# A fused attention-and-feed-forward kernel on one core: lower-triangle score pieces, the first tile's h units moved, and the last two output tiles from seven block products

## The chip, the cores and the metric

The kernel runs on one core of a Trainium2 chip. The metric is the device time of one execution in microseconds; the time before is 1198.16 us, the median of 8 runs (1196.76 to 1198.74). One further execution was taken with the hardware profiler on; its trace is what is read here.

## The reference, cut to what matters

```python
# u, v: (8, 3008, 256); z: (8, 3008, 64); w_in: (256, 2048); w_out: (2048, 256); all float32
scores = (1 / S) * matmul(z, z.T)              # per batch, S = 3008; symmetric
attn   = maximum(scores, 0) ** 2               # symmetric too
x      = u * matmul(attn, v)                   # (8 * 3008, 256)
h      = x @ w_in                              # (24064, 2048)
out    = (h * cos(h)) @ w_out                  # (24064, 256)
```

## The kernel before, in words

**Slots and tiles.** Each of the 8 batches has 3008 rows, cut into 6 column blocks J of 512 (the last has 448). A slot s is one (batch, J), 48 in all. The feed-forward part works on tiles m of 512 rows of x, 48 as well (of every two batches, the first one's last block keeps 384 rows as its tile and hands 64 to the second one's, which makes 512, in the buffer `xodd`). The order of the instructions on each engine is written out by hand (`manual_schedule`); the engines run their queues in that order, and waits follow from the data and from the buffers.

**Phase a of slot s** (`phase_a`, L305; `phase_a_first`, L347, for the first three) computes the attention output of the slot: 47 pairs of matmuls for each of the two halves `dh` of the 256 columns (`emit_value`, L257). A pair's two matmuls contract 64 rows each: t = 0 uses rows 0 to 63 of the PE array (half 0), t = 1 rows 64 to 127 (half 1), into different PSUM banks. Between the value pairs lie the score groups of later slots.

**A score group** (`emit_score`, L182) is again a pair of 64-row matmuls, with z transposed as both operands: t = 0 on half 0, t = 1 on half 1, each W columns wide, into the two banks of a PSUM pair E (three such pairs in turn, `take_e`). ACT then takes max(., 0) of both (L204), DVE squares it into a piece A (L209, L212). A piece is a 512 by 512 block (J, I) of attn; two groups, h = 0 and h = 1, make one. Since attn is symmetric, only pieces with I >= J are computed (apart from the first three slots of batch 0) and the others are turned by DMA transposes (`emit_turns`, L226, on SP's queue, L244). Of a diagonal piece (I = J, `cut` at L185) the group h = 0 is computed 256 columns wide, h = 1 at full width; the two missing 128-row blocks are turned from the piece itself by two transposes (L238).

**Phase b of slot s** (`phase_b`, L565) is the feed-forward part: eight h units of tile s - 1 (`emit_h`, L396: four 128-row matmuls, then a Sin on ACT, L411, then h times cos(h) into g on DVE, L414), and between them the output y of tile s - 2. There are two buffers of g, so that g of tile m takes the place of g of tile m - 2. For most tiles (`mixed`, L418: 1 <= m < 46 and 512 rows) y is made from seven products of half-size blocks instead of eight (a Strassen-like scheme): the sums and differences s1 and g are made on POOL (`mix_early`, L424, two instructions for each of four j), s2 and s4 on DVE (`mix_late`, L431) in the next phase a, and each product (`product`, L450) is 16 matmuls 128 columns wide into one of the two banks M0 and M1, which ACT (products 1 and 5) or DVE (the others) empties. The other tiles use 64 matmuls of 256 columns (`emit_y`, L515, `store_y`, L533). The last tile's y stands after everything (`last_y`, L544): its four 128-row blocks one after the other, each copied by ACT (L554) into an output buffer o (two in turn) and stored by SP (L560, L562; the last 64 rows by ACT's queue, L563).

**The beginning** (L597 to L685): batch 0's z is turned on PE (`turn_on_pe`, L618) in six groups, and copied out of PSUM by ACT or DVE (`copy_turned`, L625). The last two groups are turned within phase a of slot 0, at its steps 4 and 8 (`turn_late`, L669, L681). After the sixth, its PSUM space becomes the third pair E. The first two h units of tile 0 stand between phases a of slots 1 and 2 (L684, L685), the other six in phase b of slot 2. w_out is loaded after slot 1 (L683), on POOL's queue behind a small instruction (`hold`, L344) that waits for that slot's sums.

Of the kernel before, what the change touches and what calls it, by code (L numbers as in the profile page):

```python
# [14 lines left out]
def kernel(  # L15
# [9 lines left out]
    nc = tc.nc  # L25
# [155 lines left out]

    def emit_score(on_dve=False, later=None):  # L182
        b, J, I, h = groups[done_groups[0]]
        done_groups[0] += 1
        cut = I == J and not (b == 0 and J < 3)  # L185
        W = 2 * P if cut and h == 0 else width(J)
        zT = zTs[b]
        e = E[take_e()]
        for t in range(2):
            k = 4 * I + 2 * h + t  # L190
            nc.tensor.matmul(  # L191
                e[:, t, 0:W],
                zT[t * H:(t + 1) * H, k * P:(k + 1) * P],
                zT[t * H:(t + 1) * H, J * CW:J * CW + W],
                start=True,
                stop=True,
            )
        key = (b, J, I)
        a = new_piece(key) if h == 0 else piece(key)
        r = rpool.tile([P, 2, CW], FP16, name="r")  # L200
        if on_dve:
            nc.vector.tensor_scalar(r[:, :, 0:W], e[:, :, 0:W], 0.0, None, ALU.max)
        else:
            nc.scalar.activation(r[:, :, 0:W], e[:, :, 0:W], AF.Relu)  # L204
        def square():
            if I > J:
                a4 = a.rearrange("p (k t j) -> p t k j", k=4, j=P)[:, 2 * h:2 * h + 2, :, :]
                r4 = r.rearrange("p t (k j) -> p t k j", j=P)
                nc.vector.tensor_tensor(a4, r4, r4, ALU.mult)  # L209
            else:  # L210
                a4 = a.rearrange("p (k w) -> p k w", w=CW)[:, 2 * h:2 * h + 2, 0:W]
                nc.vector.tensor_tensor(a4, r[:, :, 0:W], r[:, :, 0:W], ALU.mult)  # L212

        if later is None:
            square()
        else:
            later.append(square)
        if h == 0:
            return
        if cut or (I > J and (b, J, I) not in direct):  # L220
            turns.append(((b, I), key))
            turns.sort(key=lambda t: t[0])
            turn_slots[key] = pieces[key]
            pending[pieces[key]] = "held"

    def emit_turns(due, more=0):  # L226
        while turns and (turns[0][0] <= due or more > 0):
# [6 lines left out]
            if I == J:  # L234
                a4 = a.rearrange("p (k w) -> p k w", w=CW)
                for rr in range(2, 4):
                    rows = P if J * 4 + rr < NB - 1 else H
                    nc.sync.dma_start_transpose(  # L238
                        a4[:, 0:2, rr * P:rr * P + rows],
                        a[0:rows, rr * CW:rr * CW + 2 * P],  # L240
                    )
            else:
                d = new_piece((b, I, J))
                nc.sync.dma_start_transpose(d.rearrange("p (n j) -> p n j", j=P), a)  # L244
# [102 lines left out]
    def phase_a_first(s, n, extra={}):  # L347
# [16 lines left out]
        for i, (dh, k) in enumerate(steps):  # L364
# [19 lines left out]
            for _ in range(at.get(i, 0)):  # L384
                emit_score(on_dve=done_groups[0] in on_dve)
        if s == 0:
# [31 lines left out]
    def mixed(m):  # L418
        return 1 <= m < NSLOT - 2 and mwidth(m) == CW

    F = NFT // 2
    T = 2 * P

    def mix_early(m, j):  # L424
        g, f = gs[m], slice(2 * j, 2 * j + 2)
        lower = slice(F + 2 * j, F + 2 * j + 2)
        nc.gpsimd.tensor_tensor(s1[:, f, :], g[:, f, T:], g[:, lower, T:], ALU.add)  # L427
        nc.gpsimd.tensor_tensor(g[:, f, T:], g[:, f, 0:T], g[:, f, T:], ALU.subtract)  # L428

# [19 lines left out]

    def product(m, n):  # L450
        g = gs[m]
# [9 lines left out]
        }[n]  # L461
        acc = M[order_y.index(n) % 2][:, 0:T]
        for ft in range(F):
            for k in range(2):
# [5 lines left out]
                    stop=(ft == F - 1 and k == 1),  # L470
                )
        acc = acc.rearrange("p (k d) -> p k d", d=P)
        if n == 5:
            y_outs[m] = [opool.tile([P, 2, D], FP32, name="o") for i in range(2)]
            y_parts[m] = {}
        c11, c12, c21, c22 = (y_outs[m][i][:, :, d * P:(d + 1) * P] for i in range(2) for d in range(2))
        parts = y_parts[m]
        add = lambda dst, other: nc.vector.scalar_tensor_tensor(
            dst, acc, inv_s2, other, ALU.mult, ALU.add
        )  # L480
        if n in (1, 5, 6):
            parts[n] = ypool.tile([P, 2, P], FP32, name=f"p{n}")
        if n in (1, 5):
            nc.scalar.activation(parts[n], acc, AF.Copy, bias=0.0, scale=inv_s2)
        elif n == 6:
# [14 lines left out]
    def y_bank(m, k):  # L500
        if m == NSLOT - 1 and k == 3:
            return E[0][:, 0, 0:D]
        return M[k // 2][:, (k % 2) * D:(k % 2 + 1) * D]

    def y_block(m, ft, k):
        final = m == NSLOT - 1
        nc.tensor.matmul(  # L507
            y_bank(m, k),
            gs[m][:, ft, k * P:(k + 1) * P],
            w_out16[:, ft, :],  # L510
            start=(ft == 0 and (k % 2 == 0 or (final and k == 3))),
            stop=(ft == NFT - 1 and (k % 2 == 1 or k == mwidth(m) // P - 1 or (final and k == 2))),
        )
# [30 lines left out]
    def last_y(m):  # L544
        b, J = m // NC, m % NC
        for ft in range(NFT):
            y_block(m, ft, 0)
            y_block(m, ft, 1)
        for k in range(4):
            if k >= 2:  # L550
                for ft in range(NFT):
                    y_block(m, ft, k)
            o = opool.tile([P, 2, D], FP32, name="o")
            nc.scalar.activation(  # L554
                o[:, 0, :], y_bank(m, k),
                AF.Copy, bias=0.0, scale=inv_s2,
            )
            t0 = b * S + J * CW + k * P
            if k < 3:
                nc.sync.dma_start(out[t0:t0 + P, :], o[:, 0, :])  # L560
            else:
                nc.sync.dma_start(out[t0:t0 + H, :], o[0:H, 0, :])  # L562
                nc.scalar.dma_start(out[b * S - H:b * S, :], o[H:P, 0, :])  # L563

    def phase_b(s):  # L565
        y, hs = s - 2, [(s - 1, i) for i in (0, 4, 1, 5, 2, 6, 3, 7)]
        if s == 2:
            hs = [(0, i) for i in range(2, 8)] + hs
        for dh in range(len(late_sums)):
            gate_mul(s, 2 - len(late_sums), late_sums.pop(0), nc.gpsimd)  # L570
        if mixed(y):
            ys = [lambda n=n: product(y, n) for n in order_y]
        else:
            ys = [lambda i=i: emit_y(y, i) for i in range(8)]
            ys[7] = lambda f=ys[7]: (f(), store_y(y))
        n = len(hs)
        if n > 8:
            after = (1, 2, 4, 5, 7, 8, 10, 11)
        elif mixed(y):
            after = range(7)  # L580
        else:
            after = (0, 1, 2, 3, 4, 5, 6, 6)
        for i, (m, unit) in enumerate(hs):
            times_c = emit_h(m, unit)
            if not mixed(y):
# [4 lines left out]
            if mixed(y):  # L590
                times_c()
            if mixed(m) and unit >= 4:
                mix_early(m, unit - 4)
            if i in (1, 3, 5):
# [44 lines left out]
    for g in range(3, NC):  # L639
        cast_z(nc.gpsimd, g)  # L640
        if g == 3:
            load_v(0, 1)
    on_dve = ()
    squares = []
# [24 lines left out]
    def turn_late(g):  # L669
        turn_on_pe(g)  # L670
        copy_turned(g)
        if g == NC - 1:
            E.append(ppool.tile([P, 2, CW], FP32, name="E2", tag="E2"))
            e_order.insert(0, 2)
# [8 lines left out]
    nc.gpsimd.dma_start(w_out16, moe_w_out.rearrange("(k p) f -> p k f", p=P))  # L683
    for i in range(2):  # L684
        emit_h(0, i)()  # L685
    phase_a_first(2, 14)
# [65 lines left out]
```

## Time and profile before

| | |
|---|---|
| median of 8 runs | 1198.16 us (1196.76 to 1198.74) |
| the profiled execution's own time | 1199.09 us |
| its span in the trace | 1197.3 us |
| granted PE clock | 1.0 throughout |
| phase a / phase b of a full slot, late in the run | 10 to 12 us / 13 us |
| last h unit of tile 47, first of its four matmuls | 1184.30 us |
| last store issued (L562) | 1194.08 us |

The span counts from the first to the last instruction of the program; the 1.8 us between it and the execution's own time lie outside the program. PE, DVE, ACT, POOL and SP are the engines (TensorE, VectorE, ScalarE, GpSimd, SyncE); PEld is PE's weight loads, SPq and ACTq the instructions by which an engine starts DMAs. In the timeline a line has the start in us from the span's start, the length in us, engine, line of the kernel, operation, output and inputs, shape, count, and in brackets the idle time before it and what ended that.

### The profile page before, as it was taken

Reading aid. Unit: us, or ns where it says so; the run is one execution under the profiler, and the core shown is the slowest. Engines: PE = TensorE matmul, PEld = TensorE weight load, DVE = VectorE, ACT = ScalarE, POOL = GpSimd, SP = SyncE. Lnnn points to the kernel's source line nnn. Section 1 sums busy time; section 2 is a strip of 40 time slices with the busy share of each in tenths; the row PEclk is TensorE's granted clock in tenths of the full one; section 3 lists DMA queues with packets and bytes.
Section 4 is the critical chain, followed back from the end, with each engine's and each line's share of the span. In section 5 each row is a group of like instructions: output and inputs, shape, how many; then the busy total and the mean of one; then the engine's idle time right before and its main releaser. Section 6 shows DMA issues by size and latency. Waiting matters only on the chain.

```text
span 1197.3 us, 28444 instructions
## 1 busy us (share of the span) xinstructions
PE 1187.7 (99%) x11743; PEld 703.3 (59%) x11743; DVE 996.9 (83%) x1257; ACT 795.1 (66%) x923; POOL 654.0 (55%) x667
## 2 busy tenths in 40 slices
PE   8999999999999999999999999999999999999998
PEld 4456656655556556655566555665566555656566
DVE  6888887889988897888988889788888888878775
ACT  7866676667766676666676676666766666676454
POOL 3196725557466571655647556276565665535450
PEclk9999999999999999999999999999999999999999
DMA  9999999568995699946999369973798838954301
GB/s 158 170 175 149 127 145 131 101 111 135 133 144 88 120 137 152 125 82 111 151 151 128 79 104 158 168 111 69 118 164 146 120 67 119 177 109 81 62 19 54
DMA packets 467411, 145.14 MB, mean 121 GB/s; under 512 B 391760, under 2 KB 467024, under 8 KB 467280
## 3 DMA queue, kind: packets, MB, share of 16 engines
q1 hardware_dynamic: 368304, 110.11, 51.7%
q0 software_dynamic: 97440, 32.78, 27.2%
q8 instruction: 92, 1.51, 0.5%
q10 hardware_dynamic: 1536, 0.43, 0.2%
q14 instruction: 39, 0.32, 0.1%
HBM read 66.32 MB, written 24.64 MB: 76 GB/s over the span
## 4 chain that ended last, share of the span: by engine, by line
PE 95%; DMA 2%; issue 1%; ACT 1%; DVE 0%; POOL 0%; ACTq 0%; SPq 0%; POOLq 0%
PE E L403 27%; PE M L465 21%; PE M L258 20%; PE E L258 18%; PE E L191 5%; PE M L507 3%; DMA w_out<-in_moe_w_out_dram 1%; ACT r L204 1%; DMA out_dram<-o 0%; PE E L635 0%; POOL u L140 0%; ACT o L554 0%; DVE A L209 0%; DVE A L212 0%; DVE sm L270 0%
## 5 line engine op out<-in xcount | busy, mean ns | idle before, releaser
L411 ACT ACTIVATE c<-E 128x1024 f16<-128x1024 f32 (+1 forms) x384 | 385.4, 1006 | 221.4 <-PE E L403 218.9
L414 DVE SCALAR_TENSOR_TENSOR g<-E,c 128x1024 f16<-128x1024 f32 (+1 forms) x384 | 458.7, 1196 | 74.7 <-ACT c L411 74.1
L204 ACT ACTIVATE r<-E 128x512 f16<-128x512 f32 (+1 forms) x342 | 327.7, 966 | 115.2 <-PE E L191 110.2
L258 PEld LDWEIGHTS <-v 64*128 64x128 f16 x4512 | 225.4, 94 | 252.5 <-issue 19.3
L403 PE MATMUL E<-x,w_in 128*128 128x512 f16 (+1 forms) x1408 | 354.0, 375 | 0.0
L427 POOL TENSOR_TENSOR s<-g 128x512 f16<-128x512 f16 x164 | 192.3, 1172 | 172.1 <-DVE g L414 132.6
L258 PE MATMUL M<-A,v 64*128 64x512 f16 (+1 forms) x2256 | 283.3, 372 | 0.3 <-DVE sm L270 0.3
L258 PE MATMUL E<-A,v 64*128 64x512 f16 (+1 forms) x2256 | 278.0, 372 | 0.0
L428 POOL TENSOR_TENSOR g<-g 128x512 f16<-128x512 f16 x164 | 203.2, 1239 | 12.9
L403 PEld LDWEIGHTS <-w_in 128*128 128x128 f16 x1536 | 134.4, 98 | 109.3 <-issue 19.5
L209 DVE TENSOR_TENSOR A<-r 128x1024 f16<-128x1024 f16 x240 | 173.4, 734 | 20.6 <-ACT r L204 19.8
L286 POOL TENSOR_TENSOR x<-sm,uT 128x512 f16<-128x512 f32 (+1 forms) x43 | 48.6, 1130 | 244.7 <-DVE sm L270 244.5
L465 PEld LDWEIGHTS <-g 128*128 128x128 f16 x2624 | 160.3, 98 | 37.0
L465 PEld LDWEIGHTS <-s 128*128 128x128 f16 x1968 | 120.2, 98 | 27.7
L191 PE MATMUL E<-zT 64*128 64x512 f16 (+2 forms) x684 | 126.2, 362 | 2.1 <-DVE zT L630 1.1
L433 DVE TENSOR_TENSOR s<-s,g 128x1024 f16<-128x1024 f16 x82 | 93.2, 1136 | 2.1 <-POOL s L427 2.1
L212 DVE TENSOR_TENSOR A<-r 128x512 f16<-128x512 f16 (+1 forms) x102 | 79.0, 774 | 13.9 <-ACT r L204 13.3
L465 PE MATMUL M<-w_mix,s 128*128 128x128 f16 x1312 | 86.6, 219 | 0.0
L465 PE MATMUL M<-w_out,g 128*128 128x128 f16 x1312 | 86.6, 219 | 0.0
L465 PE MATMUL M<-w_mix,g 128*128 128x128 f16 x1312 | 86.6, 219 | 0.0
L191 PEld LDWEIGHTS <-zT 64*128 64x128 f16 x684 | 35.6, 94 | 42.0 <-issue 4.4
L435 DVE TENSOR_TENSOR s<-g,s 128x1024 f16<-128x1024 f16 x82 | 55.9, 684 | 0.0
(55 smaller groups left out, 676.1 us busy)
## 6 DMA issues: line engine op xcount, KB each, us to landing
out_dram<-o SPq DMA_DIRECT2D x87, 256.0 KB, 2.2
v<-in_v_dram POOLq DMA_DIRECT2D x40, 256.0 KB, 7.7
u<-in_u_dram POOLq DMA_DIRECT2D x40, 256.0 KB, 4.9
A<-A SPq DMA_TRANSPOSE x207, 5.7
z<-in_z_dram POOLq DMA_DIRECT2D x14, 192.0 KB, 10.0
z<-in_z_dram POOLq DMA_DIRECT2D x14, 176.0 KB, 5.9
v<-in_v_dram POOLq DMA_DIRECT2D x8, 192.0 KB, 11.0
u<-in_u_dram POOLq DMA_DIRECT2D x8, 192.0 KB, 4.0
```

The lines of the kernel that those rows point to most:

```text
L191: nc.tensor.matmul(e[:, t, 0:W], zT[t * H:(t + 1) * H, k * P:(k + 1) * P], zT[t * H:(t + 1) * H, J * CW:J * CW + W], start=True, stop=True,)
L204: nc.scalar.activation(r[:, :, 0:W], e[:, :, 0:W], AF.Relu)
L209: nc.vector.tensor_tensor(a4, r4, r4, ALU.mult)
L212: nc.vector.tensor_tensor(a4, r[:, :, 0:W], r[:, :, 0:W], ALU.mult)
L258: nc.tensor.matmul(bank[:, 0:width(J)], vs[b, k // 4][t * H:(t + 1) * H, k % 4, dh * P:(dh + 1) * P], value_rhs(b, J, k, t), start=start, ...
L403: nc.tensor.matmul(e[:, f, 0:W], w_in16[:, k, ft * P:(ft + 1) * P], x[:, k, 0:W], start=(k == 0), stop=(k == 1),)
L411: nc.scalar.activation(c[:, :, 0:W], e[:, :, 0:W], AF.Sin, bias=half_pi, scale=inv_s2)
L414: return lambda: nc.vector.scalar_tensor_tensor(gs[m][:, 2 * i:2 * i + 2, 0:W], e[:, :, 0:W], 1.0, c[:, :, 0:W], ALU.mult, ALU.mult)
L427: nc.gpsimd.tensor_tensor(s1[:, f, :], g[:, f, T:], g[:, lower, T:], ALU.add)
L428: nc.gpsimd.tensor_tensor(g[:, f, T:], g[:, f, 0:T], g[:, f, T:], ALU.subtract)
L433: nc.vector.tensor_tensor(s2[:, f, :], s1[:, f, :], g[:, f, 0:T], ALU.subtract)
L465: nc.tensor.matmul(acc[:, k * P:(k + 1) * P], left[:, ft, k * P:(k + 1) * P], right[:, ft, :], start=(ft == 0 and k == 0), stop=(ft == F - ...
```

## The change

1. **Diagonal pieces** (`emit_score`): row block t of a cut piece is computed only up to its own diagonal block: widths 128 and 256 for h = 0, 384 and 512 for h = 1 (at the end of a batch 384 and 448). ACT and DVE still work on the full width W. In every second group (h = 1, cut or not) the two halves are exchanged: t = 0 goes to half 1 and t = 1 to half 0. The order of the two instructions stays t = 0, t = 1. `emit_turns` turns three strips instead of two, with 1, 2 and 3 blocks instead of 2 and 2.
2. **The first deferred square**: the square of the score group at step 5 of slot 0 is put behind the copy of the sixth turned group.
3. **Tile 0's first two h units** move from between slots 1 and 2 into phase b of slot 2, which then has 16 h units; tile 0's eight parts of y go after units 1, 3, 5, 7, 9, 11, 13 and 14.
4. **Tiles 46 and 47** become mixed. Units 0, 4, 1 and 5 of tile 46 move from phase b of slot 47 into phase b of slot 46, behind the eight units of tile 45 (tile 44's g has been read by then); the seven products of tile 45 stand between the remaining four. Their sums are made in phases b 47 and 48, partly on DVE. `last_y` makes tile 47's seven products in the order 1, 2, 4, 5, 7, 6, 3 into M1, M0, four banks of two pairs E, and M1 again, and stores its four quarters apart.

```diff
-    def emit_score(on_dve=False, later=None):
+    def emit_score(later=None):
...
         for t in range(2):
             k = 4 * I + 2 * h + t
+            half = t if h == 0 else 1 - t
+            rows = slice(half * H, (half + 1) * H)
+            Wt = min(W, (2 * h + t + 1) * P) if cut else W
             nc.tensor.matmul(
-                e[:, t, 0:W],
-                zT[t * H:(t + 1) * H, k * P:(k + 1) * P],
-                zT[t * H:(t + 1) * H, J * CW:J * CW + W],
+                e[:, t, 0:Wt],
+                zT[rows, k * P:(k + 1) * P],
+                zT[rows, J * CW:J * CW + Wt],
...
-                for rr in range(2, 4):
+                for rr in range(1, 4):
                     rows = P if J * 4 + rr < NB - 1 else H
                     nc.sync.dma_start_transpose(
-                        a4[:, 0:2, rr * P:rr * P + rows],
-                        a[0:rows, rr * CW:rr * CW + 2 * P],
+                        a4[:, 0:rr, rr * P:rr * P + rows],
+                        a[0:rows, rr * CW:rr * CW + rr * P],
                     )
...
-                emit_score(on_dve=done_groups[0] in on_dve)
+                emit_score(later=squares if s == 0 and i == lo else None)
...
     def mixed(m):
-        return 1 <= m < NSLOT - 2 and mwidth(m) == CW
+        return 1 <= m and mwidth(m) == CW
...
     def last_y(m):
         b, J = m // NC, m % NC
-        for ft in range(NFT):
-            y_block(m, ft, 0)
-            y_block(m, ft, 1)
-        for k in range(4):
...
+        t0 = b * S + J * CW
+        ea, eb = E[take_e()], E[take_e()]
+        banks = {1: M[1], 2: M[0], 4: ea[:, 0, :], 5: ea[:, 1, :], 7: eb[:, 0, :], 6: eb[:, 1, :], 3: M[1]}
+        o = [opool.tile([P, 2, D], FP32, name="o") for i in range(2)]
+        c11, c12, c21, c22 = (o[i][:, :, d * P:(d + 1) * P] for i in range(2) for d in range(2))
+        p = {n: ypool.tile([P, 2, P], FP32, name=f"p{n}") for n in (1, 5, 6)}
+        for n in (1, 2, 4, 5, 7, 6, 3):
+            multiply(m, n, banks[n][:, 0:T])
+            acc = banks[n][:, 0:T].rearrange("p (k d) -> p k d", d=P)
+            if n == 1:
+                copy_to(p[1], acc)
+            elif n == 2:
+                add_to(c11, acc, p[1])
+                nc.sync.dma_start(
+                    out[t0:t0 + T, 0:P].rearrange("(k p) d -> p k d", p=P), c11
+                )
+            elif n == 4:
+                copy_to(c21, acc)
+            elif n == 5:
+                copy_to(p[5], acc)
+                nc.gpsimd.tensor_tensor(c12, p[1], p[5], ALU.add)
+            elif n == 7:
+                add_to(c22, acc, p[1])
+            elif n == 6:
+                add_to(c12, acc, c12)
+                add_to(p[6], acc, c22)
+                nc.vector.tensor_tensor(c22, p[6], p[5], ALU.add)
+                nc.vector.tensor_tensor(c21, p[6], c21, ALU.add)
+                store_half(m, 1, o[1])
             else:
+                for k, eng in enumerate((nc.sync, nc.scalar)):
+                    add_to(c12[:, k, :], acc[:, k, :], c12[:, k, :])
+                    eng.dma_start(out[t0 + k * P:t0 + (k + 1) * P, P:D], c12[:, k, :])
 
     def phase_b(s):
         y, hs = s - 2, [(s - 1, i) for i in (0, 4, 1, 5, 2, 6, 3, 7)]
         if s == 2:
-            hs = [(0, i) for i in range(2, 8)] + hs
+            hs = [(0, i) for i in range(8)] + hs
+        elif s == NSLOT - 2:
+            hs = hs + [(s, i) for i in (0, 4, 1, 5)]
+        elif s == NSLOT - 1:
+            hs = hs[4:]
...
+        if s == NSLOT - 1:
+            tail = {
+                0: lambda: mix_early(m, 0),
+                1: lambda: mix_early(m, 1),
+                2: lambda: mix_early(m, 2),
+                3: lambda: (mix_early(m, 3, eng=nc.vector), mix_late(m, "s2", 0), mix_late(m, "s2", 1)),
+            }
+        elif s == NSLOT:
+            tail = {
+                1: lambda: (mix_late(y, "s4", 0), mix_late(y, "s4", 1)),
+                3: lambda: (mix_early(m, 0), mix_early(m, 1)),
+                7: lambda: (
+                    mix_early(m, 2, eng=nc.vector), mix_early(m, 3, eng=nc.vector),
+                    mix_late(m, "s2", 0), mix_late(m, "s2", 1),
+                    mix_late(m, "s4", 0), mix_late(m, "s4", 1),
+                ),
+            }
+        if n == 4:
+            after = (0, 0, 1, 1, 2, 2, 3)
+        elif n == 12:
+            after = range(7)
+        elif n > 8:
+            after = (1, 3, 5, 7, 9, 11, 13, 14)
...
+            if i in tail:
+                tail[i]()
...
         if g == NC - 1:
+            squares.pop()()
             E.append(ppool.tile([P, 2, CW], FP32, name="E2", tag="E2"))
...
-    for i in range(2):
-        emit_h(0, i)()
     phase_a_first(2, 14)
```

The new `multiply`, `add_to` and `copy_to` are parts of `product`, taken out of it unchanged; `mix_early` takes the engine as an argument.

## The prediction

> **What bounds the kernel now.** I read the page first, then the timeline in the four places that the change touches, then the DMA rows.
>
> ```profile
> span 1197.3 us, 28444 instructions
> PE 1187.7 (99%) x11743; PEld 703.3 (59%) x11743; DVE 996.9 (83%) x1257; ACT 795.1 (66%) x923; POOL 654.0 (55%) x667
> PE 95%; DMA 2%; issue 1%; ACT 1%; DVE 0%; POOL 0%; ACTq 0%; SPq 0%; POOLq 0%
> ```
>
> PE is the bound, and the chain of waits is PE for 95%. In the list of waits, from 60 us to the end, PE's matmuls wait for no other engine; what it loses are the switches between 64-row and 128-row matmuls (the 0.3 to 0.4 us rows "issue" of its weight loads, twice a slot, some 0.1 us of them on PE). So a PE column saved or added in the middle counts in full, and other engines count only at the two ends. How score pairs run, in a late slot (timeline, PE):
>
> ```profile
> 1011.32 0.27 PE L191 MATMUL E<-zT 64*128 64x256 f16 x2
> 1012.56 0.38 PE L191 MATMUL E<-zT 64*128 64x512 f16 x2
> 1012.78 0.92 PE L258 MATMUL E<-A,v 64*128 64x448 f16 x8
> ```
>
> A 512-wide pair takes 0.22 us to the next pair's start (0.42 ns a column), a 256-wide one 0.11. Two matmuls of 376 ns end 0.38 after the first began: the second starts about 4 ns after the first, and the halves stream side by side.
>
> **Diagonal pieces and exchanged halves.** Removed: 128 columns on half 0 in h = 0 (54 ns), 128 in the 384-wide matmul of h = 1. Per piece half 0 has 128 + 512 columns and half 1 256 + 384: 640 on either, against 768. If each half simply ran through its own columns, 37 pieces would give 54 ns and the 8 narrow ones (576 and 640 against 704) 27 ns: 2.2 us. That is one bound. But the two matmuls of a group are issued t = 0 first, and in h = 1 t = 0 is now on half 1. After h = 0, half 1 is 54 ns behind; so the 384-wide matmul can begin only when half 1 is free, and the 512-wide one, next in the queue, begins 4 ns later though half 0 has been free for 54 ns. It ends where the 512-wide one ended before. In order, nothing is saved. And every exchange costs: half 1 is free 4 ns after half 0, the matmul on half 0 follows another 4 later, so the next value pair starts 8 ns late. 684 score matmuls are 342 groups, 171 of them exchanged: 171 x 8 = 1.4 us. That is the other bound. No row shows a matmul that overtakes one waiting for the other half; the nearest one shows order kept: at 39.02 (below) six value matmuls take 1.21 us, where six elsewhere take 0.83: the second, on half 1, waits 0.4 us for DVE's sum, and the third, whose half 0 is free, does not pass it. I take **+1.4**.
>
> The Trainium skill's page "TensorE: Matmul & The Clock Gate" (Part 3, on packing small matmuls) says that matmuls start and end strictly in program order, with starts 4 ns apart, which speaks against a saving; its page "TensorEngine Tiling (Array Packing)" (Tiling Modes, Key Properties) says that tiles operate independently, which read alone would give the saving. By the one the sum has +1.4, by the other -2.2.
>
> Relu and square keep their widths: nothing. The 45 added transposes and the longer ones: SP's L238 takes about 1.2 us each, and
>
> ```profile
> A<-A SPq DMA_TRANSPOSE x207, 5.7
> ```
>
> they land in some 6 us. In a slot of 25 us SP spends some 15 on its transposes; behind them stand turn_u and the stores of y, due half a slot later or more. The pair issued at 1024.12 belongs to a slot that starts at 1052.2. I cost them at nothing; the cover is these 20 us. Without it, a late piece would hold PE up to 6 us.
>
> **The beginning.** Timeline, slot 0:
>
> ```profile
> 10.37 0.38 PE L191 MATMUL E<-zT 64*128 64x512 f16 x2
> 11.12 0.40 PE L620 MATMUL turned_e<-id,z 128*128 128x128 f16 x4
> 11.85 0.69 DVE L209 TENSOR_TENSOR A<-r 128x1024 f16<-128x1024 f16 x1 [1.02 <-ACT r L204]
> 12.46 0.42 DVE L630 COPY zT<-turned_e 128x512 f16<-128x512 f16 x1
> 12.93 0.39 PE L191 MATMUL E<-zT 64*128 64x512 f16 x2 [1.09 <-DVE zT L630]
> ```
>
> The sixth group is turned by 11.52, but its copy waits behind the square. With the square behind it, the copy runs 11.55 to 11.97 and PE's next score starts at 12.02: 0.9 us earlier. ACT's relus, which run back to back from there to 24 us, move along; late next are v's loads, which then still land 0.9 us or more before use. Now tile 0's first h units:
>
> ```profile
> 37.19 1.90 PE L403 MATMUL E<-x,w_in 128*128 128x512 f16 x8
> 38.70 0.68 DVE L270 TENSOR_TENSOR sm<-M,sm 128x512 f32<-128x512 f32 x1
> 39.02 1.21 PE L258 MATMUL M<-A,v 64*128 64x512 f16 x6
> 40.10 1.16 POOL L683 DMA_DIRECT2D w_out<-in_moe_w_out_dram  x1
> 40.66 0.39 PE L191 MATMUL E<-zT 64*128 64x512 f16 x2 [0.42 <-DVE g L414]
> 56.54 1.05 PE L507 MATMUL M<-w_out,g 128*128 128x256 f16 x8 [0.98 <-DMA w_out<-in_moe_w_out_dram]
> ```
>
> The two units lay in a hole: slot 2's second value matmul needs M1, summed by DVE until 39.4. Without them PE idles there instead, and slot 2 still begins at 39.4 (38.5 with the 0.9). What goes is their trouble behind it: ACT's two Sins (38.29 to 40.26) and DVE's products kept two E pairs, for which scores waited 0.6 and 0.25 us. So slot 2 ends about 1.8 us earlier, at 51.9. But then the first y waits: for w_out, landed at 56.5 (55.6 if its load moves with the 0.9), and for g of unit 0, which now starts late (relus to 52.4, two sums, Sin, product: 55.6). So y starts 0 to 0.9 earlier than 56.54, with two units fewer done: 2 x 0.865 = 1.73 us of PE work stands behind it, in a stretch where PE is full to 73.7. Net **+0.8**, and up to +1.7 if w_out is bound by its DMA time (16.4 us, queues at 9 tenths) and not by its issue. The low end is -0.2: the first y also loses the 0.98 us that it waited at 56.54.
>
> **The end.** Timeline:
>
> ```profile
> 1148.14 1.03 PE L403 MATMUL E<-x,w_in 128*128 128x512 f16 x4
> 1150.26 1.22 DVE L414 SCALAR_TENSOR_TENSOR g<-E,c 128x1024 f16<-128x1024 f32 x1 [0.29 <-ACT c L411]
> 1172.52 2.36 DVE L414 SCALAR_TENSOR_TENSOR g<-E,c 128x1024 f16<-128x1024 f32 x2 [0.29 <-ACT c L411]
> 1186.42 1.23 DVE L414 SCALAR_TENSOR_TENSOR g<-E,c 128x1024 f16<-128x1024 f32 x1 [1.39 <-ACT c L411]
> 1193.24 0.38 ACT L554 ACTIVATE o<-M 128x256 f32<-128x256 f32 x1 [3.68 <-DMA out_dram<-o]
> 1194.08 0.51 SPq L562 DMA_DIRECT2D out_dram<-o  x1
> ```
>
> Before, ACT waited 3.68 us for an output buffer; that wait goes. What is late next? (a) Phase b 46: unit 8 follows at 1149.0, 9 at 1149.9, but unit 10 needs the E of unit 7, whose product ends at 1151.48: 0.8 us of waiting; unit 11 that of unit 8, 0.27 more. The 3.46 us of PE work come back in phase b 47; the 1.06 do not. Phase b 48 starts at 1171.27 + 1.06 = 1172.33. (b) From there DVE has no hole. The product of tile 46's last unit starts about 0.5 later, at 1172.85, and behind it stand: 9 products at 1.14 us (two take 2.36 with 0.08 of overlap) = 10.3; 5 additions of y46 (L478, 424 ns, 0.34 apart) = 1.7; 6 first sums of 128x512 (L212 of that shape, 0.42 alone, 0.34 apart) = 2.0; 8 sums s2 and s4 (L435, 0.68, 0.60 apart) = 4.8. That is 1191.75; PE's products 1, 2, 4, 5, 7, 6 of tile 47 fit beside it. Then 4 additions and 2 sums of 256 columns at 0.34 = 2.1: the lower half is ready at 1193.8, plus 0.3 for instructions that wait for the one before them and lose the overlap. (c) SP then issues three stores of the lower half (the last block has three, L525 to L527: 0.35, 0.51 and 0.58, with their waits 1.7 us), and behind them in its queue the upper right quarter: 1195.8. From the last store's issue to the end it took 3.2 us (1194.08 to 1197.3): 1199.0, **+1.7**. Bounds: if DVE does not bind and PE's last product at 1192.9 does, -0.6; if DVE's sums take their mean beside POOL (L433: 1136 ns, not 0.68) for the six that may meet it, +4.4. I take the uncontended rows, as POOL has almost nothing left then. PE's saving in y46 and y47 (64 matmuls of 109 ns against 7 x 0.89 us, 0.76 each) lies off this path.
>
> **Sum.** 1.4 + 0.8 + 1.7 = +3.9: a span of 1201.2. The profiled execution's own 1199.09 would be 1203.0; it stands 0.9 above the median of 1198.16, so the median becomes **1202.1** us.
>
> **Rivals.** (1) The halves overtake each other: -2.2 in place of +1.4, sum +0.3, 1198.5 us: not slower. For it: the halves stream at their own pace once out of step. Against: the idle half 0 at 39.1. It decides as soon as the 512-wide matmul of h = 1 may start before the 384-wide one. (2) DVE's queue at the end meets POOL: +4.4 for 1.7, 1204.8 us; for it: POOL's sums of tile 47 run until about 1187. (3) Turned diagonal blocks land late: seven batches with one 6 us wait would be +40; against: 20 us of lead. (4) End and beginning both at their low bounds: 1.4 - 0.2 - 0.6, 1198.8, and with (1) 1195.2 us.
>
> **Chances.** Forecast 0.52 (its own range 1199.9 to 1203.7), rival 1 0.28, rival 2 or 3 0.08, rival 4, alone or with rival 1, 0.12. A measurement of this kernel tells about 0.2%, 2.4 us, from no change. Slower by more: 0.47 of the forecast and 0.08, 0.55. Within: 0.05 of the forecast, 0.20 of rival 1, 0.05 of rival 4, 0.30. Faster: 0.08 and 0.07, 0.15. The range leaves out about 0.1 on either side: 1195.4 to 1204.0.
>
> **What would show it.** After the change: score pairs of h = 1 with 8 ns lost, or a diagonal piece 54 ns shorter over its two groups; the first y near 55.7 and phase b 2 ending near 74.8 and not 73.9; PE waiting about 1 us for g in phase b 46; DVE without a hole from 1173 on, relative to the shifted end, and SP's four stores in a row. I am wrong if halves overtake, or if PE, not DVE, ends last.

## The result, and the profile after

The changed kernel takes 1202.87 us (median of 10 runs, 1201.15 to 1203.72), the kernel before beside it 1197.97 us (28 runs): ratio 1.0038, 95% interval 1.003 to 1.0046. The forecast of 1202.1 us was met within 0.8 us, and the span of the profiled execution, 1200.9 us, within 0.3 of the forecast 1201.2. The parts of the sum were not met: they were wrong by up to 3.2 us, in both directions, and it is by luck that they cancelled.

The page of the changed kernel: span, busy time of the engines, and the shares of the chain of waits.

```profile
span 1200.9 us, 28851 instructions
PE 1187.3 (99%) x11839; PEld 735.4 (61%) x11839; DVE 1006.4 (84%) x1284; ACT 795.0 (66%) x922; POOL 666.2 (55%) x680
PE 96%; DVE 2%; ACT 1%; issue 1%; DVEq 0%; ACTq 0%
```

PE is still the bound, with the same busy time, and DVE's share of the chain is now 2%. Where the 3.6 us between the two spans lie is read from the slots: the start of each phase a or b after, less the same start before.

| stretch (start of phase a or b of a slot) | before, us | after, us | gained or lost in it |
|---|---|---|---|
| up to phase a 3 | 74.00 | 76.09 | +2.10 |
| phase a 3 | 11.30 | 11.63 | +0.32 |
| from phase b 3 to phase b 46 | 1050.54 | 1048.77 | -1.77 |
| phase b 46 to the end of the span | 61.46 | 64.41 | +2.95 |

The stretch from phase b 3 to phase b 46, the middle, loses nothing and gains in steps, all of them in phases a: 0.05 us in some, 0.08 in others, nothing in the rest. The timeline of the changed kernel shows how (PE alone, phase a 3, a diagonal piece's second group):

```profile
79.17 0.38 PE L194 MATMUL E<-zT 64*128 64x512 f16 x1
79.21 0.56 PE L258 MATMUL M<-A,v 64*128 64x512 f16 x2
79.42 0.32 PE L194 MATMUL E<-zT 64*128 64x384 f16 x1
```

In the program the 384-wide matmul comes first (t = 0, half 1), then the 512-wide one (t = 1, half 0), then the next value pair. On the chip the 512-wide one starts 0.25 us ahead of the 384-wide one, and of the two value matmuls of the second line the later one (at 79.39), which stands behind both in the program, also starts ahead of it. Each half runs through its own instructions.

At the beginning (timeline of the changed kernel; the last bracket is the idle time and what ended it):

```profile
12.00 0.39 PE L194 MATMUL E<-zT 64*128 64x512 f16 x2 [0.19 <-DVE zT L682]
37.54 0.37 PE L258 MATMUL M<-A,v 64*128 64x512 f16 x1 [1.22 <-ACT sm L269]
38.50 0.80 PE L258 MATMUL M<-A,v 64*128 64x512 f16 x5 [0.58 <-DVE sm L270]
56.91 1.05 PE L512 MATMUL M<-w_out,g 128*128 128x256 f16 x8 [1.57 <-DVE g L414]
```

The deferred square does its 0.9 us (12.93 before). From 36.3 to 38.5 PE has one matmul to do, as expected. The second of slot 2's value matmuls waits there for DVE's sum until 38.50, and the third, whose half had been free since about 37.76 (0.22 us behind 37.54), starts with it and not before: a matmul that waits for another engine holds up those behind it. Then comes what was not: the windows of PE (length, PE's busy time with instructions, the granted clock, DMA's share and rate).

```profile
36.00:38.50 2.50, 0.70 (x6) 1.00 1.22 217
39.50:40.00 0.50, 0.50 (x6) 0.51 1.06 175
40.00:42.50 2.50, 2.50 (x14) 0.50 0.90 90
42.50:43.00 0.50, 0.50 (x5) 0.58 1.22 151
```

About 1 us after PE has work again its clock falls to half. From the means of the first and the last half microsecond (0.98 and 0.84 of them at 0.5) the low stretch runs from 39.51 to 42.92 us.

At the end (timeline, PE in phase b 46, then the last products and stores):

```profile
1148.80 2.90 PE L403 MATMUL E<-x,w_in 128*128 128x512 f16 x12
1152.19 2.15 PE L403 MATMUL E<-x,w_in 128*128 128x512 f16 x8 [0.49 <-DVE g L414]
...
1191.56 1.06 PE L465 MATMUL E<-w_mix,g 128*128 128x128 f16 x16
1193.10 0.41 DVE L474 SCALAR_TENSOR_TENSOR o<-E,p 128x256 f32<-128x256 f32 x1
1193.56 1.05 PE L465 MATMUL E<-w_mix,s 128*128 128x128 f16 x16 [0.95 <-DVE o L474]
1194.72 0.42 DVE L474 SCALAR_TENSOR_TENSOR o<-E,o 128x256 f32<-128x256 f32 x1 [1.21 <-PE E L465]
1197.33 0.59 SPq L532 DMA_DIRECT2D out_dram<-o  x1
1198.04 0.51 SPq L583 DMA_DIRECT2D out_dram<-o  x1
```

Phase b 46 grew by 4.52 us, which is the 3.46 of four units and the forecast 1.06 of waiting. The new thing is at 1193.56: product 6 waits until DVE has emptied product 7 (1193.10 to 1193.51), although 7 lies in the other bank of the pair. DVE, which was to have no hole, then idles 1.21 us for product 6.

### The profile page after: what moved, and what is told of

Its sections match the earlier page's. It is cut to its first block, busy times and chain, and to the rows that moved or that the text cites. A ratio compares the mean times of both kernels' runs of the same rounds, so it can differ in the third digit from the quotient of the medians.

```text
span 1200.9 us, 28851 instructions
## 1 busy us (share of the span) xinstructions
PE 1187.3 (99%) x11839; PEld 735.4 (61%) x11839; DVE 1006.4 (84%) x1284; ACT 795.0 (66%) x922; POOL 666.2 (55%) x680
## 3 DMA queue, kind: packets, MB, share of 16 engines
q8 instruction: 92, 1.51, 0.5%
## 4 chain that ended last, share of the span: by engine, by line
PE 96%; DVE 2%; ACT 1%; issue 1%; DVEq 0%; ACTq 0%
PE E L403 27%; PE M L465 22%; PE M L258 20%; PE E L258 19%; PE E L194 5%; PE M L512 2%; ACT r L204 1%; DVE g L414 1%; PE E L687 0%; DVE sm L270 0%; DVE o L474 0%; DVE A L209 0%; DVE x L286 0%; DVE s L434 0%; DVE A L212 0%
## 5 line engine op out<-in xcount | busy, mean ns | idle before, releaser
L258 PEld LDWEIGHTS <-v 64*128 64x128 f16 x4512 | 254.1, 94 | 227.1 <-issue 23.0
L428 POOL TENSOR_TENSOR s<-g 128x512 f16<-128x512 f16 x169 | 197.2, 1167 | 172.8 <-DVE g L414 129.6
L258 PE MATMUL E<-A,v 64*128 64x512 f16 (+1 forms) x2256 | 281.2, 372 | 0.0
L429 POOL TENSOR_TENSOR g<-g 128x512 f16<-128x512 f16 x169 | 208.2, 1232 | 13.3
L465 PEld LDWEIGHTS <-g 128*128 128x128 f16 x2752 | 167.8, 98 | 38.8 <-DVE g L414 1.1
L465 PEld LDWEIGHTS <-s 128*128 128x128 f16 x2064 | 125.9, 98 | 29.9 <-issue 1.7
L194 PE MATMUL E<-zT 64*128 64x512 f16 (+4 forms) x684 | 131.8, 356 | 0.6 <-ACT zT L680 0.3
L465 PE MATMUL M<-w_out,g 128*128 128x128 f16 x1376 | 91.0, 219 | 0.7 <-DVE g L414 0.6
L194 PEld LDWEIGHTS <-zT 64*128 64x128 f16 x684 | 40.4, 94 | 35.8 <-issue 2.4
```

What stands on the lines that cost most here:

```text
L194: nc.tensor.matmul(e[:, t, 0:Wt], zT[rows, k * P:(k + 1) * P], zT[rows, J * CW:J * CW + Wt], start=True, stop=True,)
L258: nc.tensor.matmul(bank[:, 0:width(J)], vs[b, k // 4][t * H:(t + 1) * H, k % 4, dh * P:(dh + 1) * P], value_rhs(b, J, k, t), start=start, ...
L428: eng.tensor_tensor(s1[:, f, :], g[:, f, T:], g[:, lower, T:], ALU.add)
L429: eng.tensor_tensor(g[:, f, T:], g[:, f, 0:T], g[:, f, T:], ALU.subtract)
L465: nc.tensor.matmul(acc[:, k * P:(k + 1) * P], left[:, ft, k * P:(k + 1) * P], right[:, ft, :], start=(ft == 0 and k == 0), stop=(ft == F - ...
```

## The experiments

None of the twelve kernels leaves any of the output out. Ratios are to the kernel before, with 95% intervals; the stretches are those of the table above.

| run | ratio (interval) | start of phase a 3, us | phase b 46 to the end, us |
|---|---|---|---|
| before, its trace | 1 | 74.00 | 61.46 |
| changed kernel | 1.0038 (1.003 to 1.0046) | 76.09 | 64.41 |
| e1_halves | 0.9992 (0.9983 to 1.0001) | 72.76 | 60.84 |
| e2_square | 0.9997 (0.9989 to 1.0006) | 72.93 | 61.24 |
| e3_start | 1.003 (1.0019 to 1.0041) | 76.09 | 61.08 |
| e4_end | 1.0033 (1.002 to 1.0045) | 73.23 | 64.24 |
| e5_cut_only | 1.0004 (0.9995 to 1.0014) | 74.04 | 60.83 |
| e6_exchange_only | 0.9997 (0.9988 to 1.0007) | 72.80 | 61.26 |
| e7_filled | 1.003 (1.0018 to 1.0041) | 74.58 | 64.41 |
| e8_banks | 1.0031 (1.0018 to 1.0043) | 75.03 | 63.66 |
| e9_best | 0.9979 (0.9971 to 0.9988) | 73.20 | 60.80 |
| e10_two_units | 0.9995 (0.9986 to 1.0004) | 72.34 | 62.81 |
| e11_act_store | 0.9997 (0.9988 to 1.0006) | 72.07 | 62.74 |
| e12_old_end | 1.0004 (0.9995 to 1.0014) | 74.36 | 60.83 |

**A caution for the third column.** With the old beginning phase a 3 starts anywhere from 72.76 to 74.04 (before, e1, e4, e5, e6). What differs is in good part the first y's wait for w_out, whose load took 16.4 us from issue to landing in the trace of before and 13.6 in e1: the wait was 0.98 us before, 0.6 in e5, none that shows in e1 and e6. The rest lies ahead of it (in e5 the sixth group is turned 0.49 us later than in e1). The trace that the forecast was made from had the longest wait of all.

**Diagonal pieces: e1, e5, e6.** e1 is part 1 alone:

```diff
+            half = t if h == 0 else 1 - t
+            rows = slice(half * H, (half + 1) * H)
+            Wt = min(W, (2 * h + t + 1) * P) if cut else W
...
-                for rr in range(2, 4):
+                for rr in range(1, 4):
```

> The kernel before with part 1 alone (the shorter diagonal matmuls, the exchanged halves and the three turned strips); the output is computed in full. Theory A, read from the trace of after (slots lose 0.05 to 0.08 us each behind phase a 3): the two halves run at their own pace, a matmul whose half is free starts ahead of an earlier one that waits for the other half, and each diagonal piece saves about 54 ns. Expected: 1.8 to 2.2 us less than before, ratio 0.9982 to 0.9985, phases a with a diagonal piece 0.05 us shorter. Theory B, step 1 of the prediction: starts keep program order, nothing is saved and 171 exchanges cost 8 ns each: 1.4 us more, ratio 1.0012.

e5 has `half = t` in place of the exchange:

> The kernel before with the diagonal matmuls cut (128 and 256 columns for h = 0, 384 and 512 for h = 1) and the third strip turned, but without the exchange: t = 0 stays on half 0. Theory A (each half runs at its own pace): half 1 still has 256 + 512 columns of a diagonal piece, as before, so nothing is saved: slot starts behind phase a 3 move by under 0.2 us in all against before; time as before within 0.3 us. Theory B (a pair's end and the next pair's start go by program order and by the sum of columns): up to 2.2 us less.

e6 has `Wt = W`, and two strips as before:

> The kernel before with the exchange alone (in h = 1, t = 0 on half 1 and t = 1 on half 0), all widths as before. Theory A (halves at their own pace): nothing, slot starts behind phase a 3 move by under 0.2 us in all. Theory B (step 1 of the prediction, 8 ns for each of 171 exchanged groups): the slots grow by 0.03 us each and by 1.4 us in all, ratio 1.0012.

By the phases of the traces theory A holds in all three; the ratios alone could not tell. In e1 the phases a shrink by the same steps as in the changed kernel, 1.83 us in all. In e5 nothing shrinks: half 1 still has its 768 columns. In e6 no phase changes by more than 0.003 us, so 171 exchanges cost nothing. Cut and exchange only pay together.

e1's ratio is less than its trace promises, and two things came with part 1 that neither theory had. In two phases b (those that end near 512 and 1050 us) PE loses 0.14 and 0.35 us; in the second DVE idles 0.61 us before it empties the last product, where it idled 0.25 before, and starts 0.45 us after PE's last matmul of it instead of 0.10, with nothing in the trace that it waits for. This is there, alike within 0.001 us, in every kernel with the cut and the old beginning (e1, e5, e9, e10, e11), and in no other. Its cause was not found. And the old end became 0.2 to 0.6 us shorter: in e1, e5 and e12 ACT waits 1.57 us for the store of the last output's first block, and not 3.3 to 3.7 as in before, e2, e3 and e6. The three have the 45 added transposes ahead of it on SP; why that shortens it was not tried.

**The beginning: e2, e3, e7, e12.** e2 is the deferred square:

```diff
-                emit_score(on_dve=done_groups[0] in on_dve)
+                emit_score(later=squares if s == 0 and i == lo else None)
...
+            squares.pop()()
```

> The kernel before with the deferred square alone (in slot 0, the last turned copy of z goes ahead of DVE's square); the two h units of tile 0 stay between phases a of slots 1 and 2. Theory A: the first 0.9 us, seen as PE's score at 12.0 in place of 12.93, last to the end, as PE has no hole large enough behind it: 0.9 us less, ratio 0.9992. Theory B: the gain is eaten by the first y, which waits for w_out (landed at 56.5 before) 0.9 us longer: 0 to 0.3 us less, ratio 0.9998 to 1.0.

PE waits 0.19 us for the copy where it waits 1.09 in e1, and phase a 3 starts at 72.93, with a wait of 0.41 us for w_out ahead of it. Its time can't be told from no change; both theories' conditions were met in part, and which one applies changes with w_out's landing.

e3 adds the moved units:

```diff
-            hs = [(0, i) for i in range(2, 8)] + hs
+            hs = [(0, i) for i in range(8)] + hs
...
-    for i in range(2):
-        emit_h(0, i)()
```

> The kernel before with parts 2 and 3 (deferred square, and the first two h units of tile 0 moved from between phases a of slots 1 and 2 to phase b of slot 2); the rest as before. Theory A: the moved units leave PE idle for 2 to 3 us near 36 to 38.5 us, the granted clock then falls to some 0.67 for about 3.5 us, and phase a 3 starts 2.1 us later than before, at about 76.1; the end 2.1 to 2.4 us later, ratio 1.0018 to 1.0020. Against the kernel with the deferred square alone the moved units then cost some 3.0 us. Theory B, steps 2 and 3 of the prediction: +0.8 us, ratio 1.0007, clock at 1.0.

Theory A: the clock falls as in the changed kernel and phase a 3 starts at 76.09. The ratio of 1.003 is above both theories'; the 0.98 us that the first y waited in the trace of before, longer than in any other, would account for it (that execution, of 1199.09 us, stands 1.4 above the median beside e3). Against e2 the moved units cost 3.6 us up to phase b 46 (1138.32 against 1134.76).

e7 fills the hole of the changed kernel:

```diff
+    spare = E[e_order[0]]
+    for i in range(10):
+        nc.tensor.matmul(spare[:, i % 2, :], warm[:, 0:P], warm, start=True, stop=True)
     phase_a_first(2, 14)
```

> The kernel after with ten further 512-wide matmuls of the warm-up's operands put ahead of phase a of slot 2, into a PSUM pair that the next score overwrites; they are computed for nothing and fall into the hole of PE at 36.1 to 38.5 us. Theory A (the low granted clock behind the hole comes from the idle time): the clock stays at 1.0 between 38.5 and 47 us, score pairs there start 0.22 apart and not 0.43, relus of tile 0's last unit end about 1.2 us earlier, phase a 3 starts at about 74.9 instead of 76.09, and the whole takes 1.2 us less than after. Theory B (the low clock has another cause, or the rest of the beginning hides it): the clock falls again or phase a 3 starts within 0.3 us of 76.09; time as after.

The windows of e7, in the columns of above:

```profile
36.00:38.50 2.50, 2.50 (x16) 1.00 1.24 217
40.00:42.50 2.50, 2.50 (x26) 1.00 1.06 91
```

The clock stays, PE gets 26 matmuls done where it got 14, and phase a 3 starts 1.51 us earlier. So the fall goes with the hole. But the hole is not enough: e8 and e12 have the same hole, unfilled, and there the clock stayed. The windows of e12:

```profile
36.00:38.50 2.50, 0.70 (x5) 1.00 1.17 185
40.00:42.50 2.50, 2.50 (x26) 1.00 1.11 119
```

Same busy time in the hole, but full clock behind it. Of four traces with the open hole (the changed kernel, e3, e8, e12) the clock fell in two, and it fell at this place in none of the ten others. One trace of e7 would thus prove little; its six executions say more. Those of the changed kernel lie in two groups, two at 1201.15 and 1201.31 us with a mean granted clock of 1.0, and eight from 1202.74 us on with 0.998. So do those of e12: five up to 1197.98 us (0.999 to 1.0), five from 1198.99 on (0.998); and e8's, three and three. In the first two the groups are some 1.6 us apart, about what the fall costs. All six of e7 lie between 1201.21 and 1201.86 us: the second group is gone. (One execution of e2, without this hole, stands at 1201.22 us and 0.998; why is not known.)

The traces also hint at what decides. In all four the recorded changes of the clock lie whole steps of 3.4133 us behind the first record: in the changed kernel the first is at 5.371 us, the fall 10 steps later at 39.504, the fall at the very end 350 steps behind the first at 1200.036; in e12 4.085 and, 349 steps on, 1195.336. In the step that holds the hole PE's matmuls fill 1.61 us in the changed kernel (36.09 to 39.50) and in e3 (35.85 to 39.27), and the clock falls at its end; in e12 they fill 1.70 (34.80 to 38.22), in e8 the hole is split over two steps with 3.15 and 1.88, and the clock stays. That would fit a clock that is set from the work of a whole step, with a limit of about half of one. It is a reading of four traces; no run shifted the hole against the steps.

> The kernel before with parts 1, 2 and 3, the end left as it was. Theory A (the parts are worth what their own stretches show, and they add up): +2.1 to +2.9 from the beginning and -1.8 from the diagonal pieces where the granted clock falls in the hole at 36 to 38.5 us, 1.0 to 1.5 less where it does not: -0.5 to +1.1 us against before, ratio 0.9996 to 1.0009; part 4 is then the whole of what after loses. Theory B (the parts work on each other): outside that range.

e12 is parts 1, 2 and 3 with the old end. It lies in theory A's range (1.0004), so what the changed kernel loses beyond it, 0.0034 or 4 us, is part 4; by the traces it is 64.41 - 60.83 = 3.6. The medians mix executions with and without the fall; group against group (medians 1202.91 and 1199.17, 1201.23 and 1197.58) it is 3.7 too.

**The end: e4, e8, e10, e11.** e4 is part 4 alone (the changed kernel with the lines of e1 and e3 as they were before):

> The kernel before with part 4 alone: products for tiles 46 and 47, units 0, 4, 1 and 5 of tile 46 in phase b 46, the new last output; parts 1, 2 and 3 undone. Theory A: 1.06 us of waiting in phase b 46 and about 1.2 us more at product 6 of tile 47, which waits until DVE has emptied product 7 from the other bank of the same pair, beside the step of the prediction: 2.3 to 2.9 us more than before, ratio 1.0019 to 1.0024. Theory B, the prediction's step for the end: 1.7 us more, ratio 1.0014.

From phase b 46 to the end 64.24 us, 2.78 more than before: theory A. The ratio, 1.0033, is higher still, as in e3.

e8 deals the banks so that product 6 gets one that ACT emptied long before:

```diff
-        ea, eb = E[take_e()], E[take_e()]
-        banks = {1: M[1], 2: M[0], 4: ea[:, 0, :], 5: ea[:, 1, :], 7: eb[:, 0, :], 6: eb[:, 1, :], 3: M[1]}
+        ea, eb, ec = E[take_e()], E[take_e()], E[take_e()]
+        banks = {1: M[1], 2: M[0], 4: ea[:, 0, :], 5: eb[:, 0, :], 7: ec[:, 0, :], 6: ea[:, 1, :], 3: M[1]}
```

> The kernel after with the banks of the last products dealt otherwise: three pairs E are taken, product 4 in the first, 5 in the second, 7 in the third, and 6 in the free bank of the first, which ACT has copied long before. Theory A (product 6 waited 0.95 us for DVE to empty product 7, only because both lie in one pair): product 6 runs right behind 7, DVE's idle 1.2 us ahead of the sums of product 6 goes, and from the start of phase b 47 to the end it is about 1.0 to 1.2 us shorter (36.4 to 36.6 us instead of 37.6); time about 1.1 us less than after. Theory B (DVE or SP's four stores set the end anyway): within 0.3 us of after.

The timeline of e8 (product 6, and DVE and POOL ahead of its sums):

```profile
1190.52 1.82 DVE L436 TENSOR_TENSOR s<-g,s 128x1024 f16<-128x1024 f16 x2
1190.55 1.24 POOL L571 TENSOR_TENSOR o<-p,p 128x256 f32<-128x256 f32 x1 [3.90 <-ACT p L477]
1190.78 1.06 PE L465 MATMUL E<-w_mix,s 128*128 128x128 f16 x16
1196.22 0.51 SPq L583 DMA_DIRECT2D out_dram<-o  x1
```

Product 6 waits for nothing and DVE's hole is gone, so the wait was for the pair. (The deal also parts product 5 from product 4, for whose copy by ACT it waited 0.47 us in the changed kernel; that wait is gone too.) But the stretch is 0.75 us shorter, and not 1.0 to 1.2: DVE's two sums take 1.82 us where they took 1.29 in the changed kernel, and POOL's addition now runs beside them. The forecast's rival 2 stands here in small: 0.53 us. (The spans of e8 and the changed kernel are 1.8 us apart; the other 1.06 come from the beginning, where the clock stayed in e8.)

e10 has tile 0's first h units in their old place (the deferred square stays), these banks, and two units fewer in phase b 46, with y and the sums of tile 46 dealt anew between the units:

```diff
-            hs = hs + [(s, i) for i in (0, 4, 1, 5)]
+            hs = hs + [(s, i) for i in (0, 4)]
...
-            hs = hs[4:]
+            hs = hs[2:]
```

> The kernel after with the beginning's h units in their old place, the banks of the last products dealt over three pairs, and only units 0 and 4 of tile 46 moved into phase b 46 (ten units there, six in phase b 47). Theory A (step 3a of the prediction: units 10 and 11 of phase b 46 wait for DVE to read the E pair three units back): with ten units no matmul of phase b 46 waits, it grows by 1.73 us and not by 4.52, and from the start of phase b 46 to the end it takes about 62.6 us (before 61.46, after 64.4, with only the banks dealt anew 63.7). Theory B (DVE's queue from phase b 47 on sets the end whatever phase b 46 does): 63.7 us, the wait turns up as one for DVE in phases b 47 and 48.

PE's last three units of phase b 46 in e10, one group without a wait; the phase grows by 1.88 us, and it is 62.81 us to the end, near theory A (62.6):

```profile
1145.20 2.90 PE L403 MATMUL E<-x,w_in 128*128 128x512 f16 x12
1148.03 1.31 PE L258 MATMUL M<-A,v 64*128 64x448 f16 x12
```

e11 changes only the queue of one store, `(nc.sync, nc.scalar)` to `(nc.scalar, nc.scalar)`:

> The kernel of the run before this one (two units) with one more edit: both upper right quarters of the last output are stored by ACT's queue, so that the last one no longer stands behind the lower half's three stores on SP's queue. Theory A (step 3c: SP's four stores in a row set the end): the last store is issued some 0.6 us earlier, and the end is 0.4 to 0.6 us earlier than in the run before it. Theory B (the landing of the lower half's last store sets the end): less than 0.2 us.

62.74 against 62.81 us: by the number theory B. The last store is issued 0.70 us earlier, counted from phase b 46, and is then one of the lower half; it lands 61.22 us after the start of phase b 46, where the last landing of e10 came at 61.58. But from the last landing to the end it is then 1.50 us, and 1.18 in e10. So the place of the last quarter behind three stores was not what set the end, and theory B's reason, that landing, is not shown either: what SP still waits for behind it stays open.

**A faster version: e9.** Parts 1 and 2, and the last output's first two blocks copied into idle buffers:

```diff
+            if k < 2:
+                o = ypool.tile([P, 2, P], FP32, name=f"p{5 - 4 * k}")
+                block = o.rearrange("p k d -> p (k d)")
+            else:
+                o = opool.tile([P, 2, D], FP32, name="o")
+                block = o[:, 0, :]
```

> The kernel before with parts 1 and 2 (shorter diagonal matmuls, exchanged halves, deferred square), the first two h units of tile 0 left between phases a of slots 1 and 2, and the old end with one edit: the last output's first two blocks are copied into two idle buffers, so that ACT's copy of the third no longer waits 3.68 us for the store of the first. Theory A (each part is worth what its own stretch of the traces shows): 1.8 us from the diagonal pieces, 0 to 0.9 from the square (the first y may wait for w_out), about 1.2 from the end (the last copy at 1192.3 instead of 1193.55, then its store): 3 to 4 us less than before, ratio 0.9967 to 0.9975. Theory B (the end waits for something else, a store's landing say): 1.8 to 2.7 less, ratio 0.9978 to 0.9985.

0.9979: 2.2 us faster than before in the medians (1195.55 against 1197.73), and the best of all, but at theory B's value. ACT's wait is gone, and the end takes 60.80 us where e1, e5 and e12 took 60.83 to 60.84 with the wait: there ACT already waited for PE 0.88 us behind it. The copy edit gained nothing; what is left as the gain are parts 1 and 2, which alone (e1, e2) had medians 1.4 and 1.1 us below before, neither of them clear of no change.

## Why the forecast of the sum held, and its steps did not

**Step 1, the halves: wrong, and by 3.2 us.** The forecast had +1.4, the trace -1.77. The step that failed is "the 512-wide one, next in the queue, begins 4 ns later though half 0 has been free for 54 ns". A matmul that waits only for its half lets those behind it pass on the other half: 79.17 before 79.42. By the prediction's own sign ("I am wrong if halves overtake") its working for this step was wrong. The row at 39.02 was read rightly, but it shows another case: there the second matmul waits for DVE, until 39.431, and the third starts at 39.437, as at 38.50 in the changed kernel. That a wait for another engine keeps the order said nothing of a wait for a half. Rival 1's bound of -2.2 had the mechanism; the rest of it is that diagonal pieces ahead of phase b 3 lie outside this stretch. The Trainium skill's "TensorE: Matmul & The Clock Gate" (Part 3) holds that matmuls start and end strictly in program order; these runs contradict it for 64-row matmuls on different halves, and agree with "TensorEngine Tiling (Array Packing)" (Key Properties), by which tiles operate independently.

**Step 2, the beginning: the chain right, the clock missed.** The square's 0.9 and the hole came as forecast. The forecast put the end of phase b 2 near 74.8; where the clock stayed it was 74.36 (e12) and 75.03 (e8), where it fell 76.09. The fall is worth 1.5 us (e7). Another 0.32 in phase a 3 was missed too: its second value matmul needs the bank M from which ACT still copies the last y (0.40 us, less 0.08 from the diagonal piece). Without the fall the step's +0.8 was 0.4 to 1.0, and 0.32 beside it. But that is against a trace with the longest wait for w_out: in the kernels that have the square and not the moved units (e2, e9, e10, e11) phase a 3 starts at 72.07 to 73.20, so the moved units cost 1.2 us or more even at the full clock. That fall is also why the first y kept its place at 56.91 against the forecast 55.7; without it, it starts at 55.18 to 55.85 (e12, e7, e8). The Trainium skill's page "TensorE: Matmul & The Clock Gate" (Part 1, What's actually happening) tells of a free-running window of 3413 ns over PE's activity; the low stretch here, 39.51 to 42.92, is 3.41 us long, and a window that runs freely agrees with a fall in two of four traces. It names one idle window of some 3.4 us as the condition; here 2.2 us without PE work but for one matmul were enough, with 1.61 us of work in the 3.41 us ahead of the fall.

**Step 3, the end: its terms right, one wait missing.** (a) 1.06 us in phase b 46: measured 4.52 for 3.46 + 1.06. (b) DVE without a hole from 1173: true up to 1193.5. The missing term is product 6, which waited for DVE's reading of product 7 out of the same pair; from phase b 47 to the end it took 37.62 us, where the working came to 36.38 (its terms for DVE add up to 1191.65 and not 1191.75, which changes little). So +2.95 for +1.7, inside the bounds. (c) SP's four stores stood in a row as forecast, but to take the last one out of that row gained 0.07 us (e11). Transposes at nothing: right for the pieces, no phase a waits for them; but in the kernels with the cut and the old beginning two phases b are late, and with the added transposes the old end is shorter, and the cause of either is open.

**The sum.** -1.77 + 2.10 + 0.32 + 2.95 = 3.6 against 1.4 + 0.8 + 1.7 = 3.9. The sum held by luck: an error of -3.2 met errors of +1.6 and +1.25. It says little for the working: with the halves right and all else as forecast, it would have been 1198.9 us, a change not to be told from none. The medians are 4.9 us apart, the spans 3.6: in the trace of before the first y waited 0.98 us for w_out, and its execution took 1.1 us more than the median beside it (1199.09 against 1197.97). What stays open: DVE's late start in two phases b, why the old end shortens with part 1, what lies between the last landing and the end, and whether the hole's place on the clock's steps is what decides the fall.

## What to carry to other kernels

Count 64-row matmuls by the half of the array they use, not by their order, as long as none of them waits for another engine: a shorter matmul here saved only what the longer-loaded half saved, so balance the halves (cut alone 0, exchange alone 0, both 1.8 us). Before work is moved out of a place where PE would otherwise idle, ask what the clock does behind the hole, and not only what the hole itself costs. Where results leave through a pair of banks that is waited for as one, put products that are emptied at different times into different pairs.

## What the runs showed of the hardware that was not expected

- Matmuls on different 64-row halves start out of program order, here by 0.25 us (79.17 and 79.42), and once out of step stay so through whole stretches of pairs. A matmul that waits for another engine keeps the order: the next one, on a half that was free, starts 6 ns behind it (39.437 and 39.431 before).
- A hole of 2.2 us with one matmul in it was followed, 0.8 to 1.0 us after its end, by 3.41 us at half the clock in two of four traces. The clock's changes lie on steps of 3.4133 us, and the step before the fall held 1.61 us of PE work in both; 1.70 in one step was not followed by a fall (e12).
- At the very end SP looks at the stores one after the other, about 0.06 us each where they have landed; the time from the last store's issue to the end of the span went from 2.7 us (e4, 1196.58 to 1199.3) to 3.8 (e9, 1190.67 to 1194.5), so an earlier last issue is not an earlier end by as much.
